# Skip term inside the accumulation of each chunk, next transform one chunk nearer, part of the parameter split put into the loop, input loads ahead of the modulation weights

## The chip, the cores and the metric

The kernel runs on one core of one Trainium2 chip. The metric is the device time of one execution in microseconds (us). The core has a matrix engine (TensorE, PE in the rows; PEld is its loading of weights), VectorE (DVE), ScalarE (ACT), GpSimd (POOL) and a queue of DMA issues on SyncE (SP). Each engine works through its own list of instructions in order, and the lists wait for each other by semaphores.

## The reference, cut to what matters

```python
h = layernorm(x) * (1 + ca) + sa                       # x: 2048 x 512
# _A_ref: a state space layer as a long convolution
P = exp(logdA[:, :, None] * l[None, None, :])          # logdA = dt * (A_re + 1j A_im), 512 x 128
K = einsum("dn,dnl,dn->dl", Cc, P, dB).real            # kernel of each channel, 512 x 2048
y = irfft(rfft(up, 2L) * rfft(Kp, 2L))[:L] + u * Dskip # convolution, and the skip term
x = x + ga * y
# _B_ref: two dense layers with Mish, 512 -> 1792 -> 512
h = layernorm(x) * (1 + cb) + sb
x = x + gb * _B_ref(h, w1, b1, w2)
```

`sa, ca, ga, sb, cb, gb` are six rows of `silu(c) @ w_mod`. The skip term `u * Dskip` is the same as adding `Dskip[d]` to `K[d, 0]`, and this is how the kernel computes it.

## The kernel before, in words

The run has three stages. From 0 to about 243 us the kernel makes K for all 512 channels and its first transform, and meanwhile transforms the normalised input. From there to about 345 us it multiplies the two spectra and transforms back. The rest is the two dense layers.

The first stage has a preamble and a loop. The preamble turns the raw parameters of four blocks of 128 channels into rows that hold logarithms of magnitudes and angles (`params(b, stage)`, tile `raw`, VectorE nearly alone). At the end of a block `split(0, 6)` on L245 writes these rows as a rounded part (a CAST) and a rest (a subtraction) into the tile `pk`, which has one buffer; `store_pk(b)` writes `pk` to memory (`pkd`), and `load_s(b)` reads it back in another layout. Block 2 is finished by `run(params(2, 5))` on L595, ahead of the statistics of the first input tiles (`u_stats(0)`) and of `visit(0)`.

The loop on L639 goes over 32 chunks of 16 channels, as a pipeline. For chunk k: `s_ang` is a product on TensorE that gives 1024 angles per row (tile `pang`, 6 matmuls); `s_sin` makes sine and cosine of them with three activations into the tile `ec`; `s_mag` (tile `m`) and `comb` multiply in the magnitudes with five VectorE instructions; `s_kgen` multiplies two halves of `ec` with 32 small products into `pkg`, which is K of the chunk; `s_ks` copies it to `ks` on ScalarE; `s_skip` adds the skip term to four columns of `ks` on VectorE (128 x 4, tile `dtap`); `s_ka` is the next transform on TensorE (8 products into `pka`); `s_tm` copies it to `gk` on ScalarE. In round k the loop issues `s_kgen(k-1)`, `s_ang(k+3)` and `s_ka(k-3)`, then `s_ks(k-1)`, `s_sin(k+2)`, `s_tm(k-3)`, then the VectorE work of `comb(k)`, `s_skip(k-2)` and `s_mag(k+1)`. Tables `pe`, `se`, `ve`, `vt` put other work into given rounds. Every eighth round ends with `visit`, 16 products `pco` on TensorE and 16 exponentials `co` on ScalarE with a switch of tables before and after.

The order on TensorE, VectorE and ScalarE within the loop is that of the code (`follow`), and every such instruction is recorded on one of three helper lines: L120 for VectorE and ScalarE, L142 for activations, L148 for matmuls. A matmul of plain f32 data shows as two records on PE.

Tiles with one tag share buffers. The tag `ec` has three buffers of one pool, and the raw parameters of blocks 0 and 2 use it before the chunks do:

```python
raw[b] = gen.tile([P, 16, P], F32, tag="raw" if b % 2 else "ec", name=f"raw{b}", bufs=1 if b % 2 else 3)
EC[k] = gen.tile([P, 2, 16, 96], F32, tag="ec", name=f"ec{k}", bufs=3)
```

`raw[2]` and `EC[2]` are given the same buffer, before and after the change.

Of the kernel before, what the change touches and what calls it, by code (L numbers as in the profile page):

```python
# [10 lines left out]
F32 = mybir.dt.float32  # L11
# [7 lines left out]
P = 128  # L19
# [3 lines left out]
NB = D // P  # L23
# [13 lines left out]
def _constants():  # L37
    r = np.arange(32)
    s = np.arange(64)
    j = np.arange(64)  # L40
    i = np.arange(32)
    th = 2 * np.pi * ((j[None, :, None] * (4 * r[:, None, None] + 1 + 128 * s[None, None, :])) % 8192) / 8192.0
    mf = np.zeros((32, 2, 64, 2, 64))
    mf[:, 0, :, 0, :] = np.cos(th)
    mf[:, 1, :, 0, :] = np.sin(th)
    mf[:, 0, :, 1, :] = -np.sin(th)
    mf[:, 1, :, 1, :] = np.cos(th)
    mf = mf.reshape(32, P, P)
    psi = 2 * np.pi * ((i[:, None] * (4 * r[None, :] + 1)) % 128) / 128.0
    da = np.stack([np.cos(psi), -np.sin(psi)], axis=1)  # L50
    bdk = np.zeros((4, 32, 2, 32, 4))
    di = np.zeros((2, 2, 32, 32, 2))
    du = np.zeros((32, 2, 2, 64))
    for t in range(4):
        bdk[t, :, :, :, t] = da
    for t in range(2):
        di[t, :, :, :, t] = da.transpose(1, 2, 0) / 2048.0
        du[:, t, t] = da.reshape(32, 64)
    ac = np.zeros((2, 96, 16, 32))
    am = np.zeros((96, 1))  # L60
    mc = np.zeros((64, 16, NM))
    fac = np.concatenate([[32], 64 * np.arange(1, 32), np.arange(32)])
    for d in range(16):
        for part in range(4):
            ac[0, 4 * d + part, d] = np.arange(32) if part < 2 else 1
            mc[4 * d + part, d] = fac if part < 2 else np.arange(NM) >= 32
    ac[1] = -ac[0]
    ac[0, 64] = MAGIC
    am[64] = -MAGIC
    mi = mf.reshape(16, 2, 2, 2, 2, 4, 4, 2, 64).transpose(1, 8, 0, 7, 5, 3, 2, 6, 4)  # L70
    f = np.float32
    return {
        "mf": np.ascontiguousarray(mf.transpose(1, 0, 2).reshape(P, 32 * P)).astype(f),
        "mi": np.ascontiguousarray(mi.reshape(P, 32 * P)).astype(f),
        "bdk": bdk.reshape(P, 256).astype(f),
        "da": np.tile(du.reshape(64, 128), (2, 1)).astype(f),
        "di": di.reshape(P, 64).astype(f),
        "ac": np.ascontiguousarray(ac.transpose(1, 0, 2, 3)).reshape(96, 1024).astype(f),
        "am": am.astype(f),
        "mc": mc.reshape(64, 16 * NM).astype(f),  # L80
        "ident": np.eye(P, dtype=f),
    }

# [2 lines left out]
def s4_block(ctx, tc, io, out):  # L86
    nc = tc.nc
# [10 lines left out]
    gen = right.enter_context(tc.tile_pool(name="gen", bufs=2, side="right"))  # L98
# [5 lines left out]
    def follow(eng, ins):  # L104
        if eng in order:
            tc.add_manual_dep(ins.ins, order[eng].name,
                              mybir.DependencyInfo(mybir.DependencyClass.NoSync, mybir.DependencyReason.DATA),
                              reason="program order")
        order[eng] = ins.ins
# [16 lines left out]
    V, A = Ordered(nc.vector, "dve"), Ordered(nc.scalar, "act")  # L126
# [20 lines left out]
    def mm(out, lhsT, rhs, start=True, stop=True):  # L147
        follow("pe", T.matmul(out, lhsT, rhs, start=start, stop=stop))  # L148

    def load(dst, src):  # L150
        follow("sp", nc.sync.dma_start(dst, src))
# [9 lines left out]
    def bank(name):  # L161
        return psum.tile([P, 512], F32, tag="pb", name=name)
# [23 lines left out]
    load(cT, io["cT"])  # L186
    gk = []
    early = conv.tile([P, KB, 3 * D], F32, tag="gk", name="early")
    dtap = gen.tile([P, 8 * NB, 4], F32, name="dtap", bufs=1)
    nc.gpsimd.memset(dtap, 0.0)  # L190
    ac = gen.tile([96, 2, 512], F32R, name="ac", bufs=1)
    am = gen.tile([96, 1], F32R, name="am", bufs=1)
    mc = pre.tile([64, 2, 8 * NM], F32R, name="mc")
# [148 lines left out]
    PK, KS, PKA = {}, {}, {}  # L342

    def s_kgen(k):
        ec = EC[k]
        pk = PK[k] = bank(f"pkg{k}")
        for e in range(16):
            t, m = e % 4, e // 4
            o = pk[32 * t:32 * t + 32, 64 * m:64 * m + 64]
            for z in range(2):  # L350
                mm(o, ec[:, z, e, 0:32], ec[:, z, e, 32:96], start=(z == 0), stop=(z == 1))

    def s_ks(k):
        KS[k] = gen.tile([P, 256], F32, tag="ks", name=f"ks{k}", bufs=3)
        A.copy(KS[k], PK[k][:, :256])

    def s_skip(k):
        V.tensor_add(KS[k][:, 0:256:64], KS[k][:, 0:256:64], dtap[:, k])

    def s_ka(k):  # L360
        PKA[k] = bank(f"pka{k}")
        p = PKA[k].rearrange("p (r d) -> p r d", d=16)
        for m in range(4):
            for cc in range(2):
                mm(p[64 * cc:64 * cc + 64, :, 4 * m:4 * m + 4], KS[k][:, 64 * m:64 * m + 64],
                         bdk[:, cc, :], start=True, stop=True)

    def s_tm(k):
        if k == 0:
            gk.append(conv.tile([P, 32, D], F32, tag="gk", name="gk"))  # L370
        A.copy(gk[0][:, :, 16 * k:16 * k + 16], PKA[k].rearrange("p (r d) -> p r d", d=16))
# [70 lines left out]
    def u_load(n):  # L442
        XT[n] = io4.tile([P, 2, D], F32, tag="i", name=f"x{n}")
        for g in range(2):
            for s in range(2):
                nc.sync.dma_start(XT[n][64 * g:64 * g + 64, s],
                                  view(io["A_u"], 2 * (4 * n + 2 * g + s) * D, [[64 * D, 32], [D, 2], [1, D]]))
# [69 lines left out]
    def run(*lists):  # L517
        for i in range(max(map(len, lists))):
            for ops in lists:
                if i < len(ops):  # L520
                    ops[i]()
# [9 lines left out]
    load_params(1)  # L531
    load_params(2)
    load(da, io["da"])
    load(dtap[0:P:32], io["dtap"].rearrange("t (k m) -> t k m", m=4))
    load(di, io["di"])
    load(ident, io["ident"])
    run(params(0, 3))
# [5 lines left out]
    def store_pk(b):  # L543
        load(pkd[b], PKR[b].rearrange("p i e n -> p (i e n)").bitcast(F32))

    def load_s(b):
        for h in range(2):
            load(S12[(2 * b + h) % 3][0:64].bitcast(F32),
                 view(pkd, (P * b + 64 * h) * 12 * P, [[3 * P, 64], [16 * 12 * P, 4], [1, 2 * P]]))
        S3[b] = pre.tile([64, 8, P], F32R, tag="s3", name=f"s3_{b}")  # L550
        load(S3[b].bitcast(F32), view(pkd, P * b * 12 * P + 2 * P, [[3 * P, 64], [16 * 12 * P, 8], [1, P]]))

    store_pk(0)
    load_s(0)
    for k in range(0, KB, 2):
        load(early[:, k:k + 2], view(io["w_mod"], k * P * 6 * D, [[6 * D, P], [P * 6 * D, 2], [1, 3 * D]]))
    for n in range(3):
        u_load(n)
    V.on = A.on = True
    run(params(1, 0), params(2, 0))  # L560
    tables("natural_log_exp_and_others")
# [4 lines left out]
    NG = 8 * NB  # L566
    done = set()

    def step(f, *a):
        if f.__name__[:2] == "s_":  # L570
            if (f, *a) in done or not 0 <= a[0] < NG:
                return
            done.add((f, *a))
            if a[1:] == (1,):
                done.add((f, a[0]))
        f(*a)
# [15 lines left out]
    run(params(1, 5))  # L592
    store_pk(1)
    load_params(3)
    run(params(2, 5))  # L595
    run(u_stats(0))
    visit(0, {2: [lambda: step(s_mag, 0), lambda: run(comb(0))], 4: [lambda: step(s_mag, 1)]})
    store_pk(2)
    s_ang(2)


    pe, se, ve, vt = {}, {}, {}, {}

    def at(d, k, f, *a):
        d.setdefault(k, []).append((f, *a))
# [3 lines left out]
    at(ve, 3, gains)  # L609
    for b in range(NB - 1):  # L610
        at(se, 8 * b + 1, load_s, b + 1)
    at(ve, 2, params, 3, 0)
    at(ve, 5, params, 3, 2)
    at(ve, 9, params, 3, 3)
# [3 lines left out]
    for n, k, d in ((0, 4, ve), (1, 7, vt), (2, 10, ve), (3, 12, ve), (4, 15, vt), (5, 17, ve), (6, 20, ve), (7, 23, vt)):  # L618
# [3 lines left out]
        for s in range(2):  # L622
            t = k + 1 + s
# [14 lines left out]

    for k in range(NG + 1):  # L639
        tc.cur_priority = 100000 + 10000 * k  # L640
        for s in [(s_kgen, k - 1), (s_ang, k + 3), (s_ka, k - 3)] + pe.get(k, []):
            step(*s)
        for s in [(s_ks, k - 1)] + se.get(k, []) + [(s_sin, k + 2), (s_tm, k - 3)]:
            step(*s)
        own = comb(k) if 0 < k < NG else []
        if own:
            own.insert(1, own.pop())
        own.append(lambda: step(s_skip, k - 2))
        if k % 8 != 7:
            own.append(lambda: step(s_mag, k + 1))  # L650
        extra = [o for f, *a in ve.get(k, []) for o in f(*a)]
        for i, o in enumerate(own):
            o()
            for e in extra[len(extra) * i // len(own):len(extra) * (i + 1) // len(own)]:
                e()
        for f, *a in vt.get(k, []):
            run(f(*a) or [])
        if k % 8 == 7 and k + 1 < NG:
            visit(k // 8 + 1)
            step(s_mag, k + 1)  # L660
    s_skip(NG - 1)
    for f in s_ka, s_tm:
        f(NG - 2)
    for f in s_ka, s_tm:
        f(NG - 1)
    pub(1, psum)
    pub_out(1)
    V.on = A.on = False
# [239 lines left out]
```

## Time and profile before

| what | value |
|---|---|
| median of 3 runs | 714.7 us (713.07 to 715.03) |
| the profiled execution | 711.97 us, span 710.2 us, mean granted TensorE clock 0.933 |
| PE busy | 623.6 us, 88% of the span |
| PEld busy | 422.5 us, 59% |
| DVE busy | 412.4 us, 58% |
| ACT busy | 319.9 us, 45% |
| POOL busy | 5.0 us, 1% |
| chain that ended last, by engine | PE 70%, DVE 19%, DMA 4%, ACT 4%, issue 2% |

The span runs from the first to the last instruction of the trace; the 1.8 us between it and the time of that execution lie outside the trace. Busy shares are averages over three stages with different limits, so what a change in one stage is worth has to be read there.

### The profile page before, as it was taken

How to read it: one execution, taken by the hardware profiler on the slowest of the kernel's cores; microseconds unless marked ns; L12 is line 12 of the kernel's file. 1: busy time of each engine (PE TensorE's matmuls, PEld its weight loads, DVE VectorE, ACT ScalarE, POOL GpSimd, SP SyncE). 2: the span in 40 equal slices, each digit the busy share in tenths (PEclk: the TensorE clock that was granted, in tenths of full speed). 3: DMA queues.
4: the chain of work that ended last, by engine and by line, in shares of the span. 5: the costliest groups of instructions: out<-in, count | busy, mean ns of one | idle time of the engine just before them, and what ended most of it. 6: DMA issues, size and time to landing. Idle time of an engine off the chain costs nothing.

```text
span 710.2 us, 11704 instructions
## 1 busy us (share of the span) xinstructions
PE 623.6 (88%) x4784; PEld 422.5 (59%) x4784; DVE 412.4 (58%) x813; ACT 319.9 (45%) x466; POOL 5.0 (1%) x12
## 2 busy tenths in 40 slices
PE   0388898789889989999349999999999999999995
PEld 0245666556556623332138778887788868878884
DVE  8979989998978577866194242322443134441113
ACT  2487797799799535433044223322232222322220
POOL 2000000000000000000000000000000000000000
PEclk9959978979969999999679999999999999999999
DMA  7842212805232589972686230052201300020002
GB/s 195 281 148 71 90 43 79 265 34 177 90 144 100 155 230 315 301 231 90 177 238 148 49 70 1 1 118 60 60 0 30 89 1 1 0 57 4 1 1 59
DMA packets 34315, 74.63 MB, mean 105 GB/s; under 512 B 5419, under 2 KB 9903, under 8 KB 33749
## 3 DMA queue, kind: packets, MB, share of 16 engines
q1 hardware_dynamic: 33380, 72.17, 35.1%
q10 hardware_dynamic: 576, 1.05, 0.7%
q0 software_dynamic: 304, 0.66, 0.5%
q8 instruction: 38, 0.62, 0.4%
q14 instruction: 17, 0.13, 0.1%
HBM read 49.73 MB, written 24.13 MB: 104 GB/s over the span
## 4 chain that ended last, share of the span: by engine, by line
PE 70%; DVE 19%; DMA 4%; ACT 4%; issue 2%; SPq 0%; DVEq 0%; ACTq 0%
PE pm L797 22%; PE po L814 21%; DVE ec L120 6%; PE pub L148 4%; PE pz L148 4%; DVE raw L120 4%; PE pkb L148 4%; PE pkg L148 3%; PE pang L148 3%; PE pka L148 2%; PE pia L762 2%; PE pco L148 2%; DVE bst L120 2%; DVE x L120 1%; PE pua L148 1%
## 5 line engine op out<-in xcount | busy, mean ns | idle before, releaser
L797 PE MATMUL pm<-hh,w1h 128*128 128x512 f32 x448 | 142.6, 398 | 0.6 <-ACT hh L120 0.6
L142 ACT ACTIVATE mh<-pm,b 128x512 f32<-128x512 f32 x56 | 38.5, 688 | 229.7 <-PE pm L797 229.7
L120 DVE TENSOR_TENSOR mal<-mh,mah 128x512 fp32r<-128x512 f32 x56 | 38.7, 690 | 154.7 <-ACT mah L120 154.3
L797 PEld LDWEIGHTS pm<-hh,w1h 128*128 128x128 f32 x448 | 84.8, 189 | 21.6 <-ACT hh L120 1.5
L814 PE MATMUL po<-w2h,mah 128*128 128x512 f32 x224 | 89.6, 400 | 1.1 <-DVE ot L120 1.1
L797 PE MATMUL pm<-hh,w1l 128*128 128x512 f32 x224 | 88.8, 397 | 0.0
L814 PE MATMUL po<-w2l,mah 128*128 128x512 f32 x224 | 88.6, 396 | 0.0
L814 PE MATMUL po<-w2h,mal 128*128 128x512 f32 x224 | 88.5, 395 | 0.0
L148 PE MATMUL pang<-ac,s 96*128 96x512 f32 x128 | 56.1, 485 | 27.0 <-DMA s<-pkd 26.5
L120 DVE TENSOR_TENSOR ec<-ec,co 128x1024 f32<-128x1024 f32 x64 | 74.9, 1201 | 6.4 <-ACT ec L142 6.4
L148 PEld LDWEIGHTS pkg<-ec 128*32 128x32 f32 x2048 | 37.8, 119 | 32.6 <-issue 15.0
L148 PE MATMUL pkg<-ec 128*32 128x64 f32 x2048 | 43.8, 239 | 12.5 <-DVE ec L120 9.9
L120 DVE TENSOR_TENSOR y<-pkb,f 128x1024 f32<-128x1024 f32 x32 | 37.7, 1219 | 26.2 <-PE pkb L148 26.2
L814 PEld LDWEIGHTS po<-w2h,mah 128*128 128x128 f32 x224 | 42.1, 188 | 16.5 <-ACT mah L120 4.9
L148 PEld LDWEIGHTS pang<-ac,s 96*128 96x128 f32 x128 | 29.1, 228 | 36.2 <-issue 27.6
L797 PEld LDWEIGHTS pm<-hh,w1l 128*128 128x128 f32 x224 | 42.3, 189 | 10.1
L814 PEld LDWEIGHTS po<-w2h,mal 128*128 128x128 f32 x224 | 42.1, 188 | 10.2
L814 PEld LDWEIGHTS po<-w2l,mah 128*128 128x128 f32 x224 | 42.1, 188 | 9.6
L148 PE MATMUL pco<-mc,s 64*128 64x512 f32 x64 | 31.1, 634 | 12.2 <-ACT co L142 7.8
L142 ACT ACTIVATE ec<-ec,halfpi 128x1024 f32<-128x1024 f32 x32 | 37.5, 1173 | 0.0
L148 PE MATMUL pka<-bdk,ks 128*64 128x128 f32 x512 | 35.8, 284 | 0.9 <-ACT gk L120 0.9
L148 PE MATMUL pz<-y,mi 64*128 64x512 f32 x128 | 32.5, 626 | 4.1 <-DVE y L120 4.1
(97 smaller groups left out, 812.5 us busy)
## 6 DMA issues: line engine op xcount, KB each, us to landing
ud<-u SPq DMA_DIRECT2D x16, 512.0 KB, 3.4
ur<-ud SPq DMA_DIRECT2D x32, 256.0 KB, 4.3
zd<-z SPq DMA_DIRECT2D x16, 512.0 KB, 3.0
zl<-zd SPq DMA_DIRECT2D x28, 256.0 KB, 4.6
x<-in_A_u SPq DMA_DIRECT2D x32, 128.0 KB, 3.5
x<-in_A_u SPq DMA_DIRECT2D x8, 512.0 KB, 6.8
out<-ot SPq DMA_DIRECT2D x32, 128.0 KB, 2.3
w1s<-in_B_w SPq DMA_DIRECT2D x8, 448.0 KB, 6.0
```

The source lines that it names most:

```text
L120: ins = getattr(self.engine, name)(*a, **kw)
L142: follow("act", nc.scalar.activation(out, in_, f, **kw))
L148: follow("pe", T.matmul(out, lhsT, rhs, start=start, stop=stop))
L762: T.matmul(p[64 * tl:64 * tl + 64, :], di, ZL[tt, hv][:, j % 2, tl, :], start=True, stop=True)
L797: T.matmul(p, w1[wi][:, k, fs], hh[:, hi, k, :], start=(n == 0), stop=(n == 3 * KB - 1))
L814: T.matmul(PO[tt][q], a[ai][:, P * q:P * q + P], w2[wi][:, f, :], start=(f == 0 and n == 0), stop=(f == FB - 1 and n == 2))
```

## The change

Four things change, all of them in the first stage.

The skip term moves from VectorE to TensorE. `s_skip` is gone; at the end of `s_kgen` one more product adds `Dskip` to columns 0, 64, 128 and 192 of `pkg`. Its weights are the constant `dl` (4 x 128), its moving data four columns of `dtap`, now a tile of 4 x 128. `dl` is one more small load, and the memset of `dtap` is gone.

`s_ka` and `s_tm` of a chunk move one round ahead, from k-3 to k-2, so that one chunk instead of two is left behind the loop.

The last two instructions of `params(2, 5)`, the CAST and the subtraction of `split`, are taken out of the preamble (`rest[-2:]`) and issued in round 1; `store_pk(2)` follows in round 3 instead of standing behind `visit(0)`.

The loads of two of the first three input tiles stand ahead of the loads of the modulation weights (`early`) in the code. In the order on SyncE the loads of these tiles already stood ahead of both loads of `early`, and stand there unchanged.

```diff
@@ _constants
+        "dl": np.kron(np.eye(4), np.eye(1, 32)).astype(f),
@@ s4_block
-    dtap = gen.tile([P, 8 * NB, 4], F32, name="dtap", bufs=1)
-    nc.gpsimd.memset(dtap, 0.0)
+    dtap = gen.tile([4, P], F32, name="dtap", bufs=1)
+    dl = gen.tile([4, P], F32, name="dl", bufs=1)
@@ s_kgen
             for z in range(2):
-                mm(o, ec[:, z, e, 0:32], ec[:, z, e, 32:96], start=(z == 0), stop=(z == 1))
+                mm(o, ec[:, z, e, 0:32], ec[:, z, e, 32:96], start=(z == 0 and m == 0), stop=False)
+        mm(pk[:, 0:256:64], dl, dtap[:, 4 * k:4 * k + 4], start=False)
...
-    def s_skip(k):
-        V.tensor_add(KS[k][:, 0:256:64], KS[k][:, 0:256:64], dtap[:, k])
...
-    load(dtap[0:P:32], io["dtap"].rearrange("t (k m) -> t k m", m=4))
+    load(dtap, io["dtap"])
+    load(dl, io["dl"])
...
+    for n in range(2):
+        u_load(n)
     for k in range(0, KB, 2):
         load(early[:, k:k + 2], view(io["w_mod"], k * P * 6 * D, [[6 * D, P], [P * 6 * D, 2], [1, 3 * D]]))
-    for n in range(3):
-        u_load(n)
+    u_load(2)
...
-    run(params(2, 5))
+    rest = params(2, 5)
+    run(rest[:-2])
     run(u_stats(0))
     visit(0, {2: [lambda: step(s_mag, 0), lambda: run(comb(0))], 4: [lambda: step(s_mag, 1)]})
-    store_pk(2)
     s_ang(2)
...
+    at(ve, 1, lambda: rest[-2:])
+    at(se, 3, store_pk, 2)
...
-        for s in [(s_kgen, k - 1), (s_ang, k + 3), (s_ka, k - 3)] + pe.get(k, []):
+        for s in [(s_kgen, k - 1), (s_ang, k + 3), (s_ka, k - 2)] + pe.get(k, []):
             step(*s)
-        for s in [(s_ks, k - 1)] + se.get(k, []) + [(s_sin, k + 2), (s_tm, k - 3)]:
+        for s in [(s_ks, k - 1)] + se.get(k, []) + [(s_sin, k + 2), (s_tm, k - 2)]:
             step(*s)
...
-        own.append(lambda: step(s_skip, k - 2))
...
-    s_skip(NG - 1)
-    for f in s_ka, s_tm:
-        f(NG - 2)
-    for f in s_ka, s_tm:
-        f(NG - 1)
+    s_ka(NG - 1)
+    s_tm(NG - 1)
```

How this moves instructions, at three places. The first is VectorE at the end of the preamble, before the change; `raw_154` is `raw[2]`, and `BN_STATS` is the start of `u_stats(0)`.

```order
L120 TENSOR_TENSOR pk_312<-raw_152,pk_312 128x3x2x128
L120 SCALAR_TENSOR_TENSOR raw_154<-raw_154 128x128 x2
L120 TENSOR_SCALAR raw_154<-raw_154 128x128
L120 SCALAR_TENSOR_TENSOR raw_154<-raw_154 128x128
L120 CAST pk_322<-raw_154 128x3x2x128
L120 TENSOR_TENSOR pk_322<-raw_154,pk_322 128x3x2x128
L120 BN_STATS bst<-x_201 128x6 x2
```

And VectorE of the change in round 1, inside `comb(1)` (`ec_305` is `EC[1]`, `ec_439` is `EC[2]`).

```order
L121 TENSOR_TENSOR ec_305<-ec_305,co_354 128x32x31
L121 TENSOR_TENSOR ec_305<-ec_305,m_1_371 128x16x32
L121 CAST pk_500<-raw_154 128x3x2x128
L121 SCALAR_TENSOR_TENSOR ec_305<-ec_305,m_1_371 128x16x32
L121 TENSOR_TENSOR m_2_503<-co_367 128x512
L121 TENSOR_TENSOR pk_500<-raw_154,pk_500 128x3x2x128
L121 TENSOR_TENSOR ec_439<-ec_439,co_367 128x32x32
```

The two instructions that read `raw[2]` last now stand directly ahead of the first VectorE instruction on `EC[2]`. The second place is ScalarE from the end of `visit(0)` on, with the semaphores that each instruction waits for, before the change (`ec_442`, `ec_495` and `ec_547` are `EC[2]`, `EC[3]`, `EC[4]`).

```order
L145 ACT_TABLE_LOAD
L120 ACTIVATE ec_442<-pang_415 128x2x16x32 [waits DVE_49,PE_49]
L142 ACTIVATE ec_442<-pang_415 128x2x16x32
L142 ACTIVATE ec_442<-ec_442,halfpi 128x2x16x32 [waits Activation_49]
L120 COPY ks_486<-pkg_446 128x256 [waits PE_49]
L120 COPY mrow<-pmod 96x512
L120 ACTIVATE ec_495<-pang_422 128x2x16x32 [waits DVE_49]
L142 ACTIVATE ec_495<-pang_422 128x2x16x32
L142 ACTIVATE ec_495<-ec_495,halfpi 128x2x16x32 [waits Activation_49]
L120 COPY ks_545<-pkg_505 128x256 [waits PE_49]
L120 ACTIVATE ec_547<-pang_479 128x2x16x32 [waits DVE_49]
```

And of the change (`EC[2]` to `EC[4]` are `ec_439`, `ec_493`, `ec_558`).

```order
L146 ACT_TABLE_LOAD
L121 ACTIVATE ec_439<-pang_412 128x2x16x32 [waits DVE_49,PE_49]
L143 ACTIVATE ec_439<-pang_412 128x2x16x32
L143 ACTIVATE ec_439<-ec_439,halfpi 128x2x16x32 [waits Activation_49]
L121 COPY ks_484<-pkg_443 128x256 [waits PE_49]
L121 COPY mrow<-pmod 96x512
L121 ACTIVATE ec_493<-pang_419 128x2x16x32
L143 ACTIVATE ec_493<-pang_419 128x2x16x32
L143 ACTIVATE ec_493<-ec_493,halfpi 128x2x16x32 [waits Activation_49]
L121 COPY ks_556<-pkg_506 128x256 [waits PE_49]
L121 ACTIVATE ec_558<-pang_477 128x2x16x32
```

The instructions are the same; the waits of `EC[3]` and `EC[4]` for VectorE are gone, because the wait of `EC[2]` is now for a later VectorE instruction, the subtraction that reads `raw[2]`, whose buffer `EC[2]` takes. The third place is TensorE at the end of the loop, before the change (`pub` is the transform of the input that follows).

```order
L148 MATMUL pkg_2830<-ec_2698 32x64 x32
L148 MATMUL pka_2863<-bdk,ks_2755 64x32x4 x8
L148 MATMUL pub_2872<-ur_2819,mf_2561 64x512 x4
L148 MATMUL pkg_2891<-ec_2760 32x64 x32
L148 MATMUL pka_2924<-bdk,ks_2817 64x32x4 x8
L148 MATMUL pka_2940<-bdk,ks_2877 64x32x4 x8
L148 MATMUL pka_2950<-bdk,ks_2933 64x32x4 x8
L148 MATMUL pub_2960<-ur_2882,mf_2561 64x512 x4
```

And of the change.

```order
L149 MATMUL pkg_2842<-ec_2711 32x64 x32
L149 MATMUL pkg_2842<-dtap,dl 128x4
L149 MATMUL pka_2876<-bdk,ks_2830 64x32x4 x8
L149 MATMUL pub_2885<-ur_2832,mf_2574 64x512 x4
L149 MATMUL pkg_2903<-ec_2773 32x64 x32
L149 MATMUL pkg_2903<-dtap,dl 128x4
L149 MATMUL pka_2937<-bdk,ks_2890 64x32x4 x8
L149 MATMUL pka_2951<-bdk,ks_2946 64x32x4 x8
L149 MATMUL pub_2961<-ur_2895,mf_2574 64x512 x4
```

Behind each group of 32 small products stands one more, in all 32 chunks, and between the last of them and `pub` stand two transforms instead of three.

## Rows read from the trace of the kernel before

**Rows 1.** Page, part 2: busy tenths of PE and DVE in 40 slices.
```profile
PE   0388898789889989999349999999999999999995
DVE  8979989998978577866194242322443134441113
```

**Rows 2.** Chain of waits, 0 to 260 us: start us, us, what.
```profile
71.47 1.50 PE pkg L148 x61
...
140.04 1.76 PE pkg L148 x62
...
154.66 1.88 PE pkg L148 x64
...
166.68 3.58 DMA x<-in_A_u
...
181.78 1.95 PE pkg L148 x62
...
206.61 1.88 PE pkg L148 x64
...
242.06 1.10 PE pkg L148 x61
243.16 2.97 PE pka L148 x48
```

**Rows 3.** DVE timeline, 38 to 60 us: start us, us, [idle before].
```profile
38.99 0.95 DVE L120 CAST pk<-raw 128x768 fp32r<-128x768 f32 x1 [3.98 <-DMA pkd<-pk]
39.97 0.96 DVE L120 TENSOR_TENSOR pk<-raw,pk 128x768 fp32r<-128x768 f32 x1
40.85 2.46 DVE L120 BATCH_NORM_STATS2 bst<-x 128x6 f32<-128x512 f32 x4
...
45.89 0.68 DVE L120 TENSOR_TENSOR m<-co 128x512 f32<-128x512 f32 x1
...
54.89 1.22 DVE L120 TENSOR_TENSOR ec<-ec,co 128x1024 f32<-128x1024 f32 x1
...
59.87 0.16 DVE L120 TENSOR_TENSOR ks<-ks,dtap 128x4 f32<-128x4 f32 x1
59.99 0.29 DVE L120 TENSOR_TENSOR raw<-raw 128x128 f32<-128x128 f32 x1
...
61.20 2.32 DVE L120 TENSOR_TENSOR ec<-ec,co 128x1024 f32<-128x1024 f32 x2
```

**Rows 4.** ACT timeline, 47 to 60 us.
```profile
47.63 1.02 ACT L120 ACTIVATE ec<-pang 128x1024 f32<-128x1024 f32 x1 [0.48 <-PE pang L148]
...
49.45 1.15 ACT L142 ACTIVATE ec<-ec,halfpi 128x1024 f32<-128x1024 f32 x1
55.49 0.37 ACT L120 COPY ks<-pkg 128x256 f32<-128x256 f32 x1 [4.88 <-PE pkg L148]
...
58.05 1.16 ACT L142 ACTIVATE ec<-ec,halfpi 128x1024 f32<-128x1024 f32 x1
```

**Rows 5.** Timeline, 78.0 to 80.6 us: PE and PEld.
```profile
77.76 1.17 PE L148 MATMUL pkg<-ec 128*32 128x64 f32 x64
...
78.86 0.19 PEld L148 LDWEIGHTS pang<-ac,s 96*128 96x128 f32 x1
78.86 0.50 PE L148 MATMUL pang<-ac,s 96*128 96x512 f32 x1
...
79.20 0.38 PE L148 MATMUL pang<-am,s 96*128 96x512 f32 x1
...
79.42 0.63 PE L148 MATMUL pang<-ac,s 96*128 96x512 f32 x2
```

**Rows 6.** PE timeline, 204 to 258 us.
```profile
208.42 0.80 PE L148 MATMUL pang<-ac,s 96*128 96x512 f32 x1
209.01 0.63 PE L148 MATMUL pang<-am,s 96*128 96x512 f32 x1
```

**Rows 7.** Chain of waits, whole run: transposes of the dense stage.
```profile
439.43 1.75 PE pln L782 x16
```

## Prediction

> **What bounds the kernel now.** First the busy tenths in slices: DVE is full from the start to about 195 us, PE is nearly full from about 50 us to the end [rows 1]. All that the change touches lies ahead of 249 us; the two later stages run on PE and take as long as before. So I then read the chain of waits from 0 to 260 us. It is a relay. DVE carries it to 71.4 us, where the small products `pkg` of a chunk start as soon as their `comb` is done. From there PE carries three chunks to the second `visit`. Behind it DVE carries it to 140.04 us, then PE and ACT to the load of an input tile at 166.68 us, for which DVE waits; DVE to 181.78 us; PE from there through the last `visit`, from 206.61 us on almost without a gap, to the three transforms at 243.16 us [rows 2]. Seventeen of the 32 groups `pkg` are pieces of this chain: three from 71.47 us, one at 140.04, two from 154.66, three from 181.78, eight from 206.61 to 242.06 us. What is taken from DVE counts only in DVE's legs, what is given to PE only in these seventeen chunks. Last I read the DVE timeline of the preamble: DVE stands for 3.98 us ahead of the CAST of block 2, because the one buffer `pk` is still being stored for block 1 [rows 3].
>
> **The split taken out of the preamble.** Without the two instructions DVE goes on to the statistics at once. It saves the wait, 3.98 us, and defers the two, 38.99 to 40.85 us, 1.86 us; the first `m` starts at 40.05 instead of 45.89 us [rows 3]. From `m` to the first instruction on `EC[2]` it is 9.00 us (45.89 to 54.89), now with the two inside, 10.86: DVE is there at 50.91 us. But the order shows what the diff doesn't: `raw[2]` and `EC[2]` are one buffer, and ACT's activations of `EC[2]` now wait for the subtraction that reads `raw[2]` last. Before they ran from 47.63 to 50.60 us (49.45 + 1.15), 2.97 us [rows 4]. Now they start at about 50.95, and DVE, whose next instruction needs them, stands until about 53.95 us. It is 0.94 us early instead of 3.98: the wait for the store becomes a wait for ACT of 3.0 us. On ACT the copy `ks` of chunk 0 is queued behind, then `mrow` and `EC[3]`. That copy came at 55.49 us after a wait of 4.88 us for PE [rows 4], so it covers the delay; without that cover 3 us would go on to `EC[3]`. `EC[3]` was done at 59.2 us, and DVE takes it at 61.20 us less the gain [rows 3, 4], still later. Gain 0.94 us; at least 0 (if ACT is later than that), at most 1.8 (no wait, then `EC[3]` is the limit: 61.20 less 59.2 less the new product of chunk 0). I take 0.94.
>
> **The VectorE add.** 32 instructions of 128 x 4 go. From one add to the next instruction it is 0.12 us, at 59.87 us [rows 3]. In DVE's legs there are nine: two before 71.4, six between 91.5 and 139.4, one between 170.4 and 181.1 us. 9 x 0.11 = 1.0 us. The others lie beside PE and give nothing (0 to 0.12 each).
>
> **The transform one chunk nearer.** Rounds 3 to 31 hold one group `pka` as before. Behind the loop the three groups of 2.97 us become two [rows 2]: 1.0 us less on the path to `pub`. The group that comes earlier falls into round 2, where PE has just been waiting on ACT and the next `pkg` for DVE; it is hidden there, and would cost 1.0 us if DVE were no later than PE. The copy `ks` of the last chunk, about 0.4 us on ACT, is covered by the other group. Gain 1.0 us, between 0 and 1.1.
>
> **The new product on TensorE.** It is two records of 128 weight columns and 4 moving columns behind the 64 records of `pkg`, and the copy `ks` waits for it. No row of this trace shows one. Below, its records go at the pitch of those of `pkg`: 1.10 us for 64 [rows 2], 0.017 each, 0.03 us a chunk. Above, they cost what a change of product costs besides: the first `pang` behind `pkg` takes 0.34 us to the second, the second 0.22 [rows 5], so 0.12 for the change. The nearest row with full-width weights and little to move are the transposes, 16 in 1.75 us, 0.109 each [rows 7]. I take two of these, 0.22 us. At half clock (1.2 GHz) the first `pang` takes 0.59 us to the second [rows 6] against 0.34, 1.7 times; so 0.37. Of the seventeen, five show the long `pkg` of the lower clock (1.50 to 1.95 us) [rows 2]: 12 x 0.22 + 5 x 0.37 = 4.5 us. One might think that four rows of weights load faster than 128. The Trainium skill, "TensorE: Matmul & The Clock Gate", section on LDWEIGHTS, says no: the time goes by the columns, columns over 1.2 GHz in nanoseconds, 107 for 128. By it two loads are an estimated 0.21 us, the sum 0.2 us lower; no run here shows a load of four rows.
>
> **The rest at nothing.** The order of the input loads against `early` on SyncE does not change. The small load `dl` and the missing memset lie in the first microseconds, beside DVE's own work. `store_pk(2)` is issued later, and its reader is a load rounds later. The order of the w1 loads and casts shifts by a step in the second stage, where PE runs without a gap.
>
> **Sum.** -0.94 - 1.0 - 1.0 + 4.5 = +1.6 us. On the profiled execution, 711.97 us, 713.6. That execution is 2.7 us below the median of the three runs, so on the median, 714.7, it is 716.3 us.
>
> **The rivals.** A change of 0.3%, 2.1 us, is about what a measurement of this kernel can tell from no change.
>
> A, faster: the weights of the new product are loaded while `pkg` still runs. Then it costs 0.03 us, 17 x 0.035 = 0.6, and the sum is -2.3 us, 712.4. Against it: the weights of `pang` are loaded only at 78.86 us, when `pkg` is over, where `pang` begins too [rows 5]; for it: the next ones are ahead of their matmul. The skill's same page, on the queue depth, lets PE pull weight loads ahead of matmuls in flight; by this rule A holds, but the first load behind `pkg` disagrees. It decides below 0.04 us a chunk.
>
> B, slower: the new product pays the change of product on top, 0.22 + 0.12 = 0.34 us, at half clock 0.58. 12 x 0.34 + 5 x 0.58 = 7.0 us, the sum +4.1 us, 718.8. For it: both sides of `pang` show such a gap [rows 5]. Against it: `pkg` to `pang` pays one already, and the product may only move it. By "TensorEngine Tiling (Array Packing)", section on tiling modes, every change of tiling mode drains the engine; four rows, then 96, behind columns of 32 would be one change more. The two records at 0.12 us each way agree in size. B decides from about 0.25 us a chunk.
>
> C, the order doesn't show the whole wait: ACT takes `EC[2]` at its old time. Then the first term is 1.8 instead of 0.94, 715.4 us. The order speaks against it.
>
> A stretch of lower clock more or less is worth about 2 us (`pkg` 1.88 for 1.10 [rows 2], `pang` likewise) and may come with any of them; the idle of PE ahead of 71.47 us shrinks, which would take one away, but DVE then limits that leg within 0.4 us.
>
> **How the numbers follow.** Forecast with C 0.45, A 0.22, B 0.33. The forecast's own range is 714.4 to 717.5 us, with 0 to 1.8 for the split and 0.15 to 0.25 us for the product. For 8 in 10 the range takes in the points of A and B, 712.3 to 718.8. Faster by over 0.3% 0.22, within it 0.45, slower 0.33.
>
> **What would show it.** Right: no wait of DVE for `pkd`, instead one of about 3 us for ACT's `ec` near 51 us; the first `ks` on ACT near 55.7 us; `pkg` to `pang` about 0.22 us longer in every chunk at full clock; two `pka` groups ahead of the second `pub`. Wrong: if that step is 0.05 or 0.34 us instead; if ACT does not stand near 47 us; if DVE carries the chain in legs where I give it to PE, since then fewer than seventeen products count.

## The result and the profile after

| kernel | median | executions | ratio to before, 95% interval |
|---|---|---|---|
| before | 713.53 us | 20 | |
| changed | 716.13 us | 20 | 1.0041 (1.0025 to 1.0057) |

The change makes the kernel slower by 2.9 us (0.0041 x 713.5; 1.8 to 4.1 us). The forecast was +1.6 us, inside a range of -2.4 to +4.1 us around the median. The likeliest case was "within 0.3%" (0.45), and 0.41% is slower by a little more than that (0.33). The time lies between the forecast and rival B (+4.1 us). In absolute time the forecast looks better than it was: 716.13 us is 0.2 us from the 716.3 on record, but that was counted from a median of three, 714.7 us, and before has 713.53 us over 20, so the near hit is chance. The profiled execution of the changed kernel took 714.6 us with a span of 712.8 us, 2.6 us more than that of before.

The first thing to look for is the new product itself. Timeline of the changed kernel, PE and weight loads (PEld), around one chunk in the leg before the second visit; columns are start us, duration us, engine, line, operation, tiles, shape, count.

```profile
80.83 1.17 PE L149 MATMUL pkg<-ec 128*32 128x64 f32 x64
81.93 0.29 PEld L149 LDWEIGHTS pkg<-dtap,dl 4*128 4x128 f32 x2
81.94 0.38 PE L149 MATMUL pkg<-dtap,dl 4*128 4x4 f32 x2
82.24 0.19 PEld L149 LDWEIGHTS pang<-ac,s 96*128 96x128 f32 x1
82.25 0.50 PE L149 MATMUL pang<-ac,s 96*128 96x512 f32 x1
```

From the first `pkg` to the first `pang` it was 1.10 us (77.76 to 78.86, [rows 5]); now it is 1.42 (80.83 to 82.25; 1.41 before these ends are rounded). The weights of the product are loaded only when `pkg` is over (80.83 + 1.10 = 81.93), those of `pang` 0.31 us later (82.24): neither load is pulled ahead, and the step is 0.31 to 0.32 us longer. At half clock (1.2 GHz granted) it is:

```profile
207.57 1.95 PE L149 MATMUL pkg<-ec 128*32 128x64 f32 x64
209.45 0.58 PE L149 MATMUL pkg<-dtap,dl 4*128 4x4 f32 x2
209.97 0.80 PE L149 MATMUL pang<-ac,s 96*128 96x512 f32 x1
```

2.40 us from 207.57 to 209.97, where before it was 1.88 [rows 2]: 0.52 us more.

The second thing is the end of the preamble. VectorE and then ScalarE of the changed kernel, with the idle time and what ended it in brackets.

```profile
49.07 0.95 DVE L121 TENSOR_TENSOR pk<-raw,pk 128x768 fp32r<-128x768 f32 x1
53.12 1.23 DVE L121 TENSOR_TENSOR ec<-ec,co 128x1024 f32<-128x1024 f32 x1 [3.10 <-ACT ec L143]
59.30 1.22 DVE L121 TENSOR_TENSOR ec<-ec,co 128x1024 f32<-128x1024 f32 x1
```

```profile
50.11 1.02 ACT L121 ACTIVATE ec<-pang 128x1024 f32<-128x1024 f32 x1 [3.73 <-DVE pk L121]
```

The wait for the store of `pkd` is gone [rows 3]. In its place ScalarE waits 3.73 us for the subtraction that reads `raw[2]` last, and VectorE 3.10 us for ScalarE, which is the wait that the order had shown. The first `ks` came at 53.96 us, 1.7 us ahead of the forecast's 55.7, after a wait of only 0.87 us for `pkg`; this took nothing back, since VectorE reached `EC[3]` only at 59.30 us.

The third thing is the end of the loop. Chain of waits of the changed kernel, start us, us, what:

```profile
247.91 1.90 PE pka L149 x32
249.80 1.74 PE pub L149 x8
```

Two groups `pka` in 1.90 us stand where three took 2.97 [rows 2].

### The profile page after: what moved, and what is told of

It reads as the page before. It is cut to its first block, busy times and chain, and to the rows that moved or that the text cites. A ratio compares the mean times of both kernels' runs of the same rounds, so it can differ in the third digit from the quotient of the medians.

```text
span 712.8 us, 11744 instructions
## 1 busy us (share of the span) xinstructions
PE 631.1 (89%) x4848; PEld 430.5 (60%) x4848; DVE 410.3 (58%) x781; ACT 320.0 (45%) x466; POOL 4.8 (1%) x11
## 4 chain that ended last, share of the span: by engine, by line
PE 70%; DVE 19%; ACT 4%; DMA 3%; issue 2%; SPq 0%; ACTq 0%; DVEq 0%
PE pm L796 22%; PE po L813 22%; DVE ec L121 6%; PE pub L149 4%; DVE raw L121 4%; PE pz L149 4%; PE pkg L149 4%; PE pkb L149 4%; PE pang L149 3%; PE pka L149 2%; PE pia L761 2%; PE pco L149 2%; DVE bst L121 1%; ACT ec L143 1%; PE pua L149 1%
## 5 line engine op out<-in xcount | busy, mean ns | idle before, releaser
L149 PE MATMUL pang<-ac,s 96*128 96x512 f32 x128 | 54.5, 471 | 25.7 <-DMA s<-pkd 25.7
L149 PEld LDWEIGHTS pkg<-ec 128*32 128x32 f32 x2048 | 35.7, 114 | 30.0 <-issue 14.0
L149 PE MATMUL pkg<-ec 128*32 128x64 f32 x2048 | 41.6, 230 | 9.0 <-DVE ec L121 7.8
L149 PE MATMUL pka<-bdk,ks 128*64 128x128 f32 x512 | 37.4, 293 | 0.5 <-ACT gk L121 0.5
L149 PEld LDWEIGHTS pka<-bdk,ks 128*64 128x64 f32 x512 | 29.5, 145 | 11.0 <-ACT u L121 5.5
```

## The experiments

Twelve kernels, each timed in five rounds against the kernel before; times in us are the ratio less one, times 713. "Step" is the time from the first `pkg` to the first `pang` of a chunk at full clock (2.4 GHz granted). The code shows only what matters of each edit; `...` marks what is cut.

**The product alone.** The kernel before, with only this part of the change:

```diff
+        mm(pk[:, 0:256:64], dl, dtap[:, 4 * k:4 * k + 4], start=False)
...
-        own.append(lambda: step(s_skip, k - 2))
...
```

> The kernel before with the skip term as a product on TensorE, all else as before. Theory P (the product pays the change of product on top, as two steps from pkg to pang of the changed kernel read: 1.42 us at full clock where before read 1.10, 2.40 where before read 1.88): 14 chunks on the chain x 0.31 + 3 x 0.52 = 5.9 us, less 0.5 to 1.0 us for the VectorE adds: 4.9 to 5.4 us slower than before, the step pkg to pang 1.41 us at full clock. Rival Q (my forecast's size, 0.22 and 0.37 a chunk): 3.2 to 3.7 us slower, step 1.32. Rival R (the changed kernel's loss is mostly longer stretches of lower clock in its one profile): within 1.5 us of before. On the small load cT: it landed 1.4 us earlier in the changed kernel, and VectorE's preamble ran 0.78 us ahead; if that comes from the new form of the dtap load, it shows here too (first angle instruction raw near 9.2 us and not 10.0), if by chance, perhaps not.

Measured: 1.0089 (1.006 to 1.0118), 6.3 us slower, step 1.41. Theory P holds; Q's size is below the interval (4.3 to 8.4), and R falls.

**The transform alone.** The kernel before, with

```diff
-        for s in [(s_kgen, k - 1), (s_ang, k + 3), (s_ka, k - 3)] + pe.get(k, []):
+        for s in [(s_kgen, k - 1), (s_ang, k + 3), (s_ka, k - 2)] + pe.get(k, []):
...
-        own.append(lambda: step(s_skip, k - 2))
         if k % 8 != 7:
             own.append(lambda: step(s_mag, k + 1))
+        own.append(lambda: step(s_skip, k - 1))
...
```

> The kernel before with only the transform one chunk nearer. For this the VectorE add has to come one chunk earlier too, so it stands behind the magnitudes of the next chunk, for chunk k-1. Theory P: two pka groups instead of three between the last pkg and the second pub, 1.0 us faster, and nothing else changes: 1.0 us faster than before. Rival W (the add waits for the copy ks of the chunk just made, VectorE stands for it in its own legs): 0 to 2 us slower than before, with waits of ks on VectorE for ACT in the rounds where VectorE carries the chain.

Measured: 0.9998 (0.9977 to 1.0019). The order of TensorE behind the loop is as intended, two groups in 1.8 us; PE of this kernel:

```profile
246.21 1.97 PE L148 MATMUL pka<-bdk,ks 128*64 128x128 f32 x32
248.01 1.89 PE L148 MATMUL pub<-ur,mf 128*64 128x512 f32 x8
```

The time moved by -1.6 to +1.4 us, which holds P's gain of 1.0 us and no gain as well. In the one profile part of the gain is taken by rival W: from chunk 7 to the point in chunk 14 at which the chain leaves VectorE it took 44.08 us (96.93 to 141.01), before 43.47 (96.57 to 140.04), 0.61 us more, of which 0.34 is one wait of VectorE for `ks`:

```profile
100.37 0.17 DVE L120 TENSOR_TENSOR ks<-ks,dtap 128x4 f32<-128x4 f32 x1 [0.34 <-ACT ks L120]
```

Another such wait, 0.70 us at 54.98, lies in the preamble. So with the add on VectorE the nearer transform costs some of its own gain in this profile. With the product no VectorE instruction stands between `pkg` and `s_ka`: the copy `ks` holds the skip term already.

**The split alone.** The kernel before, with

```diff
+    rest = params(2, 5)
+    run(rest[:-2])
-    run(params(2, 5))
...
-    store_pk(2)
...
+    at(ve, 1, lambda: rest[-2:])
+    at(se, 3, store_pk, 2)
```

> The kernel before with only the last two instructions of block 2's split moved into round 1 and its store into round 3. Theory P (the wait for the store becomes a wait for ACT, since EC[2] takes the buffer of raw[2]): VectorE stands 3.0 to 3.1 us for ACT's ec ahead of the first instruction on EC[2], which starts 0.9 us earlier than before, 54.0 and not 54.9 us; 0.9 us faster than before. Rival C (no such wait): that instruction starts near 53.0 us, 1.8 us faster. Rival Z (VectorE's lead is taken back at TensorE or at a load in the loop): not faster, within 0.5 us of before. The VectorE preamble starts as before, first angle instruction raw near 10.0 us, if the earlier start in the changed kernel came from the form of the dtap load.

Measured: 1.0003 (0.9981 to 1.0026). The wait is there, on both engines:

```profile
49.92 1.02 ACT L120 ACTIVATE ec<-pang 128x1024 f32<-128x1024 f32 x1 [3.73 <-DVE pk L120]
```

```profile
52.92 1.23 DVE L120 TENSOR_TENSOR ec<-ec,co 128x1024 f32<-128x1024 f32 x1 [3.10 <-ACT ec L142]
```

C falls. The time is that of before (+0.2 us); the gain of 0.9 us is inside the interval (-1.4 to +1.9 us), and so is Z's nothing. The early start of the preamble (VectorE's first angle instruction on 256 columns at 8.98 us here and 9.16 in the changed kernel, 9.94 before) came here too, with the old form of the `dtap` load; it was the small load `cT` of the one profile of before that landed late, after 6.0 us in place of 4.5, not part of the change.

**Everything but the product.** The changed kernel with the add back on VectorE, for chunk k-1 as above.

```diff
-        mm(pk[:, 0:256:64], dl, dtap[:, 4 * k:4 * k + 4], start=False)
...
+        own.append(lambda: step(s_skip, k - 1))
...
```

> The changed kernel with the skip term back as an add on VectorE (for chunk k-1, behind the next magnitudes), all else as changed. Theory P (the product is the whole loss, split and transform each give about 1 us): 1.9 us faster than before, 2.7 if the earlier start of the preamble comes too. Rival Q (a smaller product): the same here, the runs with the product tell them apart. Rival Z (the gains of the early stages are taken back later): within 0.7 us of before.

Measured: 1.0049 (1.0024 to 1.0073), 3.5 us slower. All three theories missed, and the profile says why the kernel isn't what it was meant to be. The longer list `own` moved the subtraction of the split behind the first add, and the add waits for the first `ks`:

```profile
56.50 0.17 DVE L120 TENSOR_TENSOR ks<-ks,dtap 128x4 f32<-128x4 f32 x1 [7.54 <-ACT ks L120]
56.58 0.95 DVE L120 TENSOR_TENSOR pk<-raw,pk 128x768 fp32r<-128x768 f32 x1
57.45 1.22 DVE L120 TENSOR_TENSOR ec<-ec,co 128x1024 f32<-128x1024 f32 x1
```

By its waits `EC[2]` then got the buffer of `EC[0]`: ScalarE stood 6.97 us ahead of it for the first `pkg`, and for the subtraction only ahead of `EC[3]`. VectorE is at `EC[2]` at 57.45 us, 4.3 later than in the changed kernel. This run says nothing of the product.

**The product twice.** The changed kernel, and once more with zeros as moving data:

```diff
+        mm(pk[:, 0:256:64], dl, d0, start=False)
...
```

> The changed kernel with the new product issued twice in every chunk, the second time with zeros as moving data: two records more behind each pkg. In the changed kernel one product makes the step from pkg to pang 0.31 us longer at full clock. Theory M (a change of product of about 0.1 us, and two weight loads that cost 0.109 us each like those of the transposes): step 0.22 us longer than in the changed kernel, 1.63 us, and 16 chunks on the chain give 3.5 to 4.5 us more than the changed kernel, about 6.5 to 7.5 us slower than before. Rival S (each record pays its load and its product one behind the other, 0.155 us): step 1.73, 8 us slower than before. Rival N (the price is the change of product alone, further records go at 0.017 us): step 1.45, about 3.5 us slower than before.

Measured: 1.0061 (1.0039 to 1.0083), 4.4 us slower than before; step 1.63. PE of one chunk:

```profile
224.48 1.17 PE L149 MATMUL pkg<-ec 128*32 128x64 f32 x64
225.58 0.38 PE L149 MATMUL pkg<-dtap,dl 4*128 4x4 f32 x2
225.82 0.36 PE L149 MATMUL pkg<-d,dl 4*128 4x4 f32 x2
226.11 0.50 PE L149 MATMUL pang<-ac,s 96*128 96x512 f32 x1
```

The step is that of theory M: two further records cost 0.22 us (1.63 - 1.41), so of the 0.31 us of the one product 0.09 is left for the change of product, if the first two records cost as much as the next two. The total is less than M said, by 2 us.

**The product in other shapes.** The changed kernel, with `dtap` and `dl` padded by zero rows to 128 and the product in four pieces (128 x 32, the shape of `pkg`); the second with the padded rows only (128 x 128); the third in four pieces without padding (4 x 32).

```diff
-        mm(pk[:, 0:256:64], dl, dtap[:, 4 * k:4 * k + 4], start=False)
+        for t in range(4):
+            mm(pk[32 * t:32 * t + 32, 0:256:64], dl[:, 32 * t:32 * t + 32], dtap[:, 4 * k:4 * k + 4], start=False)
...
```

> The changed kernel with the skip term as four products in the shape of pkg (128 rows, of which 4 are not zero, by 32 weight columns, 4 moving columns), so eight records more, none with 128 weight columns. Theory P (the price of the new product is its full-width weights and the change of shape; records in the shape of pkg go at their pitch, 0.017 us): step from pkg to pang 0.14 us longer than before, 1.24 us at full clock and not 1.41; 16 x 0.17 = 2.7 us less than the changed kernel, within 1 us of before. Rival F (any further product behind pkg pays the same, since its accumulation must wait for the last of pkg): step 1.41 or longer, as slow as the changed kernel, about 3 us over before.

> The changed kernel with the new product over 128 rows, of which 4 are not zero, by 128 columns, in place of 4 rows by 128 columns: two records as in the changed kernel. Theory R (the change to four rows is what costs): step from pkg to pang 1.15 to 1.25 us at full clock, about level with before. Rival K (two full-width weight loads one behind the other cost it, whatever the rows): step 1.41 as in the changed kernel, about 3 us slower than before.

> The changed kernel with the new product as four of 4 rows by 32 columns: eight records of 32 weight columns, but of 4 rows. Theory R (the change of rows costs): step from pkg to pang 1.35 to 1.45 us at full clock, about 3 us slower than before. Rival K (the weight columns cost): step 1.14 to 1.2 as with 128 rows by 32 columns, level with before or 1 us faster.

| product: rows x weight columns, records | step | ratio to before |
|---|---|---|
| none (before) | 1.10 | 1 |
| 128 x 32, 8 | 1.14 | 0.9982 (0.9964 to 1.0001) |
| 4 x 32, 8 | 1.27 | 0.999 (0.9973 to 1.0006) |
| 128 x 128, 2 | 1.34 | 1.0012 (0.9995 to 1.0029) |
| 4 x 128, 2 (changed) | 1.41 | 1.0041 (1.0025 to 1.0057) |
| 4 x 128, 4 (twice) | 1.63 | 1.0061 (1.0039 to 1.0083) |

The rows behind it, of 128 x 32, of 128 x 128 and of 4 x 32 in turn:

```profile
223.17 1.11 PE L149 MATMUL pkg<-ec 128*32 128x64 f32 x62
224.03 0.11 PEld L149 LDWEIGHTS pkg<-dtap,dl 128*32 128x32 f32 x1
224.09 0.20 PEld L149 LDWEIGHTS pkg<-dtap,dl 128*32 128x32 f32 x6
224.31 0.50 PE L149 MATMUL pang<-ac,s 96*128 96x512 f32 x1
```

```profile
220.76 1.17 PE L149 MATMUL pkg<-ec 128*32 128x64 f32 x64
221.86 0.30 PEld L149 LDWEIGHTS pkg<-dtap,dl 128*128 128x128 f32 x2
222.08 0.19 PEld L149 LDWEIGHTS pang<-ac,s 96*128 96x128 f32 x1
222.10 0.48 PE L149 MATMUL pang<-ac,s 96*128 96x512 f32 x1
```

```profile
221.70 1.17 PE L149 MATMUL pkg<-ec 128*32 128x64 f32 x64
222.80 0.15 PEld L149 LDWEIGHTS pkg<-dtap,dl 4*32 4x32 f32 x8
222.97 0.50 PE L149 MATMUL pang<-ac,s 96*128 96x512 f32 x1
```

Eight records in the shape of `pkg` cost 0.04 us; the first two of their loads even lie among the last loads of `pkg` (at 224.03 and 224.06 us). Two records of 128 columns cost 0.24 us over 128 rows and 0.31 over four. So both the columns and the change of rows cost: two records of 128 columns 0.20 more than eight of 32 (0.14 at four rows), four rows 0.07 more than 128 (0.13 at 32 columns). Neither R nor K is the whole: both missed the step of both runs. In the first run F falls, and P's step, 1.24, was 0.10 too long. The Trainium skill, "TensorE: Matmul & The Clock Gate", section on LDWEIGHTS, has loads go by columns and not by rows. The load records agree (0.29 us for two over four rows, 0.30 over 128); the steps do not, 0.31 against 0.24: the load of `pang` follows the first load of the product by 0.22 us over 128 rows (221.86 to 222.08) and by 0.31 over four (81.93 to 82.24).

**The same shape without the rest.** The kernel before, with the product in the shape of `pkg` and no add.

> The kernel before with the skip term as four products in the shape of pkg and the VectorE add gone; transform, split and loads as before. It gives the worth of the add. Theory P (nine adds of 0.11 us on VectorE's legs, less 0.04 us for each of 17 chunks): 0.3 us faster than before; the version that has transform and split too was 1.3 us faster, so those would be worth 1 us. Rival A (the transform and the split are worth nothing by themselves, as their single runs read, and the add is the whole gain): 1.3 us faster.

Measured: 1.0022 (1.0008 to 1.0036), 1.6 us slower. Both theories missed in sign: taking the add off VectorE gains nothing. Set beside the version with this product and the rest of the change (-1.3 us), it prices transform and split together at 2.9 us (1.2 to 4.5, from the two intervals); the product alone (+6.3) set beside the changed kernel (+2.9) gives 3.4 us (1.1 to 5.8). Both intervals hold the 2.1 us that the rows of split (1.0) and transform (1.1) give, and rule out that the two give nothing, which their single runs don't.

**The split earlier.** The changed kernel, with

```diff
     run(u_stats(0))
+    run(rest[-2:])
...
-    at(ve, 1, lambda: rest[-2:])
```

> The changed kernel with the two moved instructions of the split put right behind the statistics of the first tiles, ahead of the second stage of the preamble, and not into round 1. Theory P (the wait of VectorE for ACT's ec near 50 us exists only because the subtraction that frees the shared buffer was put so late): ACT takes EC[2] near 46.5 us, VectorE does not wait for it; the next limit is EC[3], which ACT has at about 57.7 us behind the copy ks of chunk 0, so VectorE starts on EC[3] near 57.7 and not 59.3 us: 1.6 us faster than the changed kernel, about 1.3 us slower than before. Rival C (EC[3] comes earlier as well): the whole 3.0 us, level with before. Rival Z (the lead is taken back in TensorE's leg or at a load): as the changed kernel, 3 us slower than before.

Measured: 1.0038 (1.002 to 1.0055), as the changed kernel. The place answers as P said, VectorE waits only for `EC[3]`, at 57.67 and not 59.30 us:

```profile
57.67 2.33 DVE L121 TENSOR_TENSOR ec<-ec,co 128x1024 f32<-128x1024 f32 x2 [1.36 <-ACT ec L143]
```

The lead is 1.16 us at chunk 14 (137.47 against 138.63 us) and gone at chunk 15 (153.18 against 152.90). Windows from 139 to 142 us with the busy time of PE, PEld, DVE, ACT and POOL; PEclk, the granted clock as a share of 2.4 GHz, is the third value from the end. First the changed kernel, then this one:

```profile
139.00:142.00 3.00, 3.00 (x68) 2.37 (x59) 2.86 (x9) 1.87 (x4) 0.00 (x0) 1.00 0.34 99
```

```profile
139.00:142.00 3.00, 3.00 (x22) 2.43 (x14) 2.96 (x5) 2.02 (x4) 0.00 (x0) 0.50 0.10 24
```

In this execution the lead was spent on a stretch at the lower clock, 1.2 GHz, which the changed kernel's profile hasn't at that place. Over the timed executions the time is that of the changed kernel (+2.7 against +2.9 us), with intervals wide enough to hide P's 1.6. Whether the earlier arrival brings the lower clock on was not told apart.

**Both good parts.** The shape of `pkg` and the early split together.

> The changed kernel with both: the skip term as four products in the shape of pkg, and the split's last two instructions right behind the statistics. Theory P (the lead of 1.6 us at EC[3] reaches the end): 1.2 to 1.6 us faster than the version with the shape alone, 2.5 to 2.9 us faster than before. Rival Z (the lead is taken back behind the second visit, by more time at the lower clock, as with the early split in the changed kernel, which led by 1.16 us at chunks 5 to 14 and by nothing from chunk 16 on): level with the version with the shape alone, about 1.3 us faster than before.

Measured: 0.9962 (0.9934 to 0.9989), 2.7 us faster than before, the fastest version. It is 1.4 us below the shape alone, which is P's size, but the intervals overlap.

**No product, early split.** The changed kernel with the early split, and with the VectorE add for chunk k-1 in place of the product.

> No product: skip term as VectorE add for chunk k-1 behind the next magnitudes, transform one chunk nearer, the split's last two instructions right behind the statistics, loads as changed. In the run without the product the subtraction was placed behind the add, EC[2] got the buffer of EC[0] and waited for the first pkg; here it is ahead of all chunks, so EC[2] has its old buffer. Theory P: 0.9 + 1.6 us in the preamble and 1.0 us behind the loop, 3.5 us faster than before. Rival Z (the gains ahead of the first visit and behind the loop do not reach the end): within 1.5 us of before, as the runs with one of them alone. Rival W (the nearer add makes VectorE wait): slower than before.

Measured: 0.9976 (0.9955 to 0.9997), 1.7 us faster. It can't be P, since the preamble gains nothing: the first nearer add waits 6.09 us for `ks`, and VectorE is at `EC[2]` at 56.34 us, later than before (54.89).

```profile
56.25 0.17 DVE L120 TENSOR_TENSOR ks<-ks,dtap 128x4 f32<-128x4 f32 x1 [6.09 <-ACT ks L120]
```

Where this version's 1.7 us come from stays open.

## Why the prediction held, and which terms were off

**The split: right.** From the first `m` to the first instruction on `EC[2]` I had 13.90 us (40.05 to 53.95); measured 13.92 (39.20 to 53.12). Both ends lie 0.8 us earlier than forecast, because the forecast was counted from the profile of before, in which `cT` landed late. In six profiles with the split in round 1 that instruction stands at 52.92 to 53.22 us; with the old place at 53.65 and 54.62 us in the two versions with a product, and 54.1 in before without that late landing (54.89 - 0.78). The mean gain is 1.0 us, forecast 0.94. The old wait, for a store, varies: 3.67 us in one of the two versions, 4.49 in the other and 3.98 before. Rival C is refuted: the wait for ScalarE is 3.10 us in all six.

**The VectorE add: wrong.** I counted nine adds of 0.11 us on VectorE's legs, 1.0 us. The leg from chunk 7 to chunk 14 holds six of them and took 43.47 us before (96.57 to 140.04) and 43.51 after (95.12 to 138.63); in the profiles with a product alone 43.52 and 43.52 us. What was given back is in the order of VectorE. The other work of a round is dealt out between the entries of `own`, and with one entry fewer more of it stands ahead of the last instruction of `comb`. VectorE in `comb(14)`, its first and its last instruction and what stands right ahead of the last, in the kernel before:

```profile
133.40 1.22 DVE L120 TENSOR_TENSOR ec<-ec,co 128x1024 f32<-128x1024 f32 x1
...
139.02 0.17 DVE L120 TENSOR_SCALAR rsq<-mv 128x4 f32<-128x4 f32 x1
139.22 0.17 DVE L120 TENSOR_SCALAR rstd<-rsq 128x4 int32<-128x4 int32 x1
139.30 0.68 DVE L120 SCALAR_TENSOR_TENSOR ec<-ec,m 128x512 f32<-128x512 f32 x1
```

And in the changed kernel:

```profile
131.74 1.22 DVE L121 TENSOR_TENSOR ec<-ec,co 128x1024 f32<-128x1024 f32 x1
...
137.21 0.16 DVE L121 TENSOR_SCALAR rsq<-mv 128x4 f32<-128x4 f32 x1
137.40 0.17 DVE L121 TENSOR_SCALAR rstd<-rsq 128x4 int32<-128x4 int32 x1
137.61 0.17 DVE L121 TENSOR_SCALAR rsq<-rsq 128x4 f32<-128x4 f32 x1
137.81 0.16 DVE L121 TENSOR_TENSOR rsq<-rstd,rsq 128x4 f32<-128x4 f32 x1
137.89 0.68 DVE L121 SCALAR_TENSOR_TENSOR ec<-ec,m 128x512 f32<-128x512 f32 x1
```

Four small instructions, each waiting for the one before, stand there in place of two, and `comb(14)` takes 6.15 us from the first to the last instruction in place of 5.90. Ahead of it the removed adds had brought only 0.21 us (96.57 to 133.40, 36.83 us, against 95.12 to 131.74, 36.62). The step that failed was to price nine adds by the row of one, without reading what stands around the others and how the rest of VectorE's list moves. Two of the six adds of this leg cost nothing, as here in the kernel before and in the changed one:

```profile
132.08 0.68 DVE L120 SCALAR_TENSOR_TENSOR ec<-ec,m 128x512 f32<-128x512 f32 x1
132.68 0.16 DVE L120 TENSOR_TENSOR ks<-ks,dtap 128x4 f32<-128x4 f32 x1
132.79 0.69 DVE L120 TENSOR_TENSOR m<-co 128x512 f32<-128x512 f32 x1
```

```profile
130.41 0.68 DVE L121 SCALAR_TENSOR_TENSOR ec<-ec,m 128x512 f32<-128x512 f32 x1
131.12 0.69 DVE L121 TENSOR_TENSOR m<-co 128x512 f32<-128x512 f32 x1
```

From the last instruction of `comb` to `m` it is 0.71 us with the add and without it; so it is at 118.43 us too (116.71 in the changed kernel). A third add, at 113.59 us, cost 0.08: 0.68 us with it (112.99 to 113.67) against 0.60 (111.34 to 111.94). At the other three the order around the add changes too, so they can't be priced one by one.

**The transform: right.** 1.90 us for 2.97, 1.07 us less, forecast 1.0. Without the product one profile shows 0.61 us of it lost again in VectorE's leg; the time of that run, -0.1 us (-1.6 to +1.4), doesn't settle it.

**The product: the mechanism was right and the size too small.** I took 0.22 us a chunk, the two loads alone, and left the change of product, 0.12, to rival B, on the ground that `pkg` to `pang` pays one already. It pays another: 0.31 us at full clock and 0.52 at half, against B's 0.34 and 0.58. The 0.22 for the loads themselves holds, as the product issued twice shows; the term that I put at nothing is the change. In the changed kernel the chain lists seventeen groups `pkg` again. One, at 124.45 us, leads to a tile's load for which VectorE, at work without a gap, does not stand; of the other sixteen two are at half clock, so 14 x 0.31 + 2 x 0.52 = 5.4 us in place of 4.5. The leg that both profiles run at full clock throughout shows that the steps add up: from `pkg` of chunk 24 to that of chunk 31 it took 28.27 us before (213.72 to 241.99) and 30.10 now (216.33 to 246.43), 1.83 more for the six of its seven chunks behind which TensorE does not wait. Rival A's overlap does not happen in this shape; in the shape of `pkg` it does, and that version's -1.3 us (-2.6 to +0.1) holds A's -2.3. The range held because it took in both rivals; the forecast itself was 1.3 us short, since its two errors, 1.0 at the add and 0.9 at the product, point the same way.

**The sum.** In us: -1.0 (split) - 0 (add) - 1.1 (transform) + 5.4 = +3.3 us; measured +2.9 (1.8 to 4.1). A straight line through the five shapes, weighted by their intervals, gives -2.1 us (standard error 0.6) at a step like that of before, and 13.1 us (2.0) for each microsecond of step. The first is what split and transform make by the rows, 2.1; the second is somewhat fewer than the sixteen chunks, and the doubled product shows it most. Why some of the added time doesn't reach the end isn't settled. The runs of single parts fit the sum only within their intervals, or at their edge: product alone 6.3 against 5.4, transform and split each 0 against -1, shape alone 1.6 against 0.6.

## What to carry to other kernels

Of the four shapes tried here, a small product that is added to an accumulation was cheap only in that of the products around it: 0.04 us for eight padded records against 0.31 for two compact ones, and the whole change came to -1.3 us (-2.6 to +0.1) in place of +2.9 (1.8 to 4.1). Price such a product by the step between its neighbours and count the change of shape on both sides. When an instruction is taken out of a list that deals other work between its entries, read the new order first, since the removal can be given back there, and look whether the instruction stood in a pause that stays without it; and when a last reader is moved later, look up who inherits its buffer.

## What was not expected of the hardware

One kernel's executions differ by more than the change is worth: those of before run from 709.85 to 718.43 us in 35. A part is seen in the granted clock, whose stretches at the lower level lie differently in each profile. From 30 to 71 us it is 0.79 of 2.4 GHz before and 1.00 in the changed kernel; from 155 to 166 us it is the other way round. Windows of before and then of the changed kernel:

```profile
155.00:166.00 11.00, 11.00 (x224) 7.77 (x217) 9.81 (x16) 10.01 (x15) 0.00 (x0) 0.89 0.34 97
```

```profile
155.00:166.00 11.00, 11.00 (x118) 7.69 (x120) 8.01 (x12) 7.02 (x11) 0.00 (x0) 0.72 0.29 66
```

From `pkg` of chunk 15 to that of chunk 16 it took 5.96 us in the one profile (154.59 to 160.55) and 8.79 in the other (152.90 to 161.69), of which 0.52 is the product. The rest does not need the product: it took 8.57 us with the split alone (152.05 to 160.62; 0.53 of full clock from 152 to 161 us) and 8.41 with the transform alone (154.97 to 163.38). In all profiles but that of before it took 7.3 to 9.4 us; whether 5.96 is the rule for the kernel before can't be told from its one profile. A forecast made from one profile, of terms of a microsecond, has to be checked on medians, while the step inside a chunk, at full clock and where TensorE doesn't wait, repeats to about 0.02 us (1.08 to 1.10 before, 1.39 to 1.41 changed).
